# Head outputs of groups 0 to 5 stored by token and brought back through DMA transposes; partial value products from two terms

## The chip, the core and the metric

The kernel runs on one core of a Trainium2 chip, in one launch. The metric is the device time of that launch in microseconds (us). TensorE (PE) does the matmuls and the weight loads before them (PEld), VectorE (DVE) and ScalarE (ACT) do elementwise work, GpSimd (POOL) hardly works here, and SyncE (SP) issues every DMA.

## The reference

```
xn = layernorm(x)                                  # x: 2048 tokens x 640
q, k, v = split(xn @ wqkv)                         # 32 heads of 20
p = softmax(q k^T / sqrt(20))                      # no mask, 2048 x 2048 per head
s = concat_heads(p @ v) @ wo
u = gelu(einsum("sd,sf->df", layernorm(xn), w1) + b1)   # a perceptron over tokens, F = 1536
g = silu((u @ w2 + b2)^T)
out = x + s * g
```

All tensors are bf16.

## The kernel before

**A planner writes the order.** `schedule()` runs when the kernel is built. It keeps an estimated clock for every engine, and at each step appends one instruction to one engine's list, the best candidate by priority and estimated readiness. Every instruction names the slots that it reads and writes, and `_add` (L81) turns these into semaphore waits. So the order on each engine is fixed at build time, and an engine that waits holds up all that stands behind it on its list. All DMAs stand on SP's list. They take eight semaphores ("lanes") in turn, and a DMA also waits for the one before it on its lane, which is the eighth DMA back (L171).

**Passes.** The heads are cut into 8 groups of 4, the queries into 4 blocks of 512. Groups 0 to 5 run as passes 0 to 23, four passes each; groups 6 and 7 alternate in passes 24 to 31. A pass has 16 key chunks x 4 heads, which makes 64 tiles of scores, 128 keys x 512 queries each; the whole run has 2048. PE computes a tile into one PSUM bank (L1114). The exponential of it is taken by one of two engines:

- ACT (L1143) takes two or three banks in one instruction and writes `pt_sb`.
- DVE takes four tiles of one key chunk at a time. L1154 turns each into an integer that is read as a bf16 power of two, and L1178 adds three constants to all four, so that there are four terms whose weighted sum approximates the exponential. The weights sit in the values: `v_sb` for term 0 and the scaled copies `vs_sb` for terms 1 to 3.

The value products (L1194) gather a pass in PSUM bank 6, 21 rows per head (a row of ones gives the denominator). A tile from ACT costs one value product, a tile from DVE four. `emit_pv` may take all terms of a DVE chunk that are left, or, with `PARTS = (2, 1)`, two or one of them as soon as these are ready:

```
for n in self.PARTS:
    if n < left or (n == left and not whole):
        pv.append(mk([], [(quads[0], n)]))
```

How many tiles go to DVE is not set anywhere: the planner gives DVE a chunk when DVE's estimated clock has room. In this kernel it is 480 tiles of 2048.

**End of a pass** (`ep_steps`, L1283). Four DVE instructions: L1288 transposes bank 6 in blocks of 32x32 into `tr_sb`, so that tokens lie on partitions; L1294 takes the reciprocal of the denominators; L1299 multiplies and writes `on_sb` (one buffer); L1301 transposes `on_sb` back into a slot of `stage_sb`. SP then stores the slot to the scratch `oT_scratch_dram`, 128 KB in rows of one feature (L1305).

**Reload.** When pass 23 is done, ten DMAs (L802) bring the 480 features of groups 0 to 5 into `oT_sb`, which is the space of `xnT_sb`. Groups 6 and 7 are brought back pass by pass. The output projection (L829, and L834 for the last block) reads `oT_sb` as weights, a block of tokens at a time, from pass 26 on; L844 multiplies with the gate, L854 adds x, L863 stores. The four last token blocks are done after the last pass (L1453, L1455, L1457, L1460).

**Work between the passes.** The projections for later groups, the perceptron and its elementwise steps are jobs that the planner sets between tiles of scores when their planned pass has come. The second matmul of the perceptron (L557 with `regB`) takes `w2` in eight pieces of 768 KB, loaded into two halves of `regA` (L693): a piece can be loaded once PE is through with the piece two before it, and PE waits for it when it comes to it. The SP list around the reload is: store of pass 23, ten reload DMAs, a `w2` piece, store of pass 24, four small reloads, a `w2` piece, and so on.

**Other lines that the prediction names.** L440 loads the second bias by single elements: 2048 pieces of 2 bytes. L583 stores projected q and k from the three slots of `qs_sb`, L622 loads them by head for the next group. L1209 is a filler matmul that adds zeros, put in where the planner expects PE to sit idle.

Of the kernel before, what the change touches and what calls it, by code (L numbers as in the profile page):

```python
# [10 lines left out]
P = 128  # L11
# [235 lines left out]
class _Kern:  # L247
    D = 640
    H = 32
    DH = 20  # L250
# [30 lines left out]
    NTILE, NLIVE, EARLY = 8, 3, True  # L281
    QC = ((0.5, 3.0), (3.2, 6.4), (9.0, 13.5), (14.0, 18.0), (19.0, 22.0))
    LAG_D, LAG_J = 99.0, 99.0
    PARTS = (2, 1)
    V1A, V1B = 0.8, 4.0

    def __init__(self, nc, A_x, A_wqkv, A_wo, B_w1, B_b1, B_w2, B_b2, out):
# [13 lines left out]
    def build(self):  # L301
        nc = self.nc
        pr = self.prog
        S, NB, FC = self.S, self.NB, self.FC
        es = ExitStack()
        with es:
            E = es.enter_context
            bf, f32, u16 = dt.bfloat16, dt.float32, dt.uint16
            t = {}

            def sb(name, shape, d):
                t[name] = E(nc.sbuf_tensor(name, shape, d))
# [12 lines left out]
            sb("pt_sb", [P, self.RP, 512], bf)  # L325
            sb("dt_sb", [P, self.NTILE, 4, 512], u16)
            sb("zt_sb", [P, 2, 2, self.D], bf)
            sb("tr_sb", [P, 512], f32)
            sb("on_sb", [P, 16, 32], bf)
            sb("rden_sb", [P, 16], f32)  # L330
            sb("stage_sb", [P, 3, 512], bf)
            sb("idb_sb", [P, P], bf)
            sb("zw_sb", [P, 32], bf)
            sb("bst_sb", [P, NB, 12], f32)
            sb("st_sb", [P, 8, NB], f32)
            sb("cst_sb", [P, 4], f32)
            sb("b1h_sb", [P, FC], f32)
            sb("b2h_sb", [P, NB], f32)
            sb("bload_sb", [P, FC + NB], bf)
            t["ps_all"] = E(nc.psum_tensor("ps_all", [P, 4096], f32))  # L340
            t["qk_dram"] = nc.dram_tensor("qk_scratch_dram", [2, 560, S], bf)
            t["oT_dram"] = nc.dram_tensor("oT_scratch_dram", [8 * P, S], bf)
            sems = {}
            for e in ("pe", "act", "dve", "pool", "sp"):
                sems[e] = E(nc.semaphore(f"sem_{e}"))
            for i in range(pr.n_lanes):
                sems[f"d{i}"] = E(nc.semaphore(f"sem_d{i}"))
            self.t = t
            self.schedule()
            pr.final_waits()  # L350
            pr.emit(sems)

    def schedule(self):
# [10 lines left out]
        idb_sb, bst_sb, st_sb, cst_sb = t["idb_sb"], t["bst_sb"], t["st_sb"], t["cst_sb"]  # L364
        b1h_sb, b2h_sb, bload_sb = t["b1h_sb"], t["b2h_sb"], t["bload_sb"]
        ps_all, oT_dram, qk_dram, qs_sb = t["ps_all"], t["oT_dram"], t["qk_dram"], t["qs_sb"]
        PROW = 4096
        A_x, A_wqkv, A_wo, B_w1, B_b1, B_w2, B_b2, out = (self.A_x, self.A_wqkv, self.A_wo, self.B_w1,
                                                          self.B_b1, self.B_w2, self.B_b2, self.out)
# [425 lines left out]
        def oT_loads(f0, f1, col0, n, rd, wr, nm):  # L795
            steps = []
            for (c, r, h, o, nh, m) in pieces(f0, f1):
                d = oT_sb[r:r + nh * m, c, col0:col0 + n]
                sr = bass.AP(oT_dram, (32 * h + 1 + o) * S + col0, [[32 * S, nh], [S, m], [1, n]])
                ws = S_(f"{wr}_{c}_{r}")  # L800
                oT_slots.setdefault((wr, c), []).append(ws)
                steps.append(("dma", lambda e, d=d, sr=sr: e.dma_start(d, sr), rd, [ws], f"{nm}_{c}_{r}", nh * m * n * 2, xall))  # L802
            return steps

        xall = [S_(f"xT{dc}_{gb}") for dc in range(5) for gb in range(4)]

        def reload_steps():
            return oT_loads(0, 480, 0, S, [S_(f"oTd{G}") for G in range(6)], "oTa", "oTload") + [("tag", "oT")]

        def reload6_steps(p):  # L810
            def make(bk):
# [471 lines left out]
        def ep_steps(q):  # L1283
# [6 lines left out]
            def okacc():  # L1290
# [7 lines left out]
            nout = bass.AP(on_sb, 1, [[512, P], [32, 16], [1, DH]])  # L1298
            steps.append(("dve", lambda e: e.tensor_tensor(nout, nin, rin, ALU.mult), [S_("tr"), S_("rden")],  # L1299
                          [S_("on")], f"epm{q}", dv(320)))  # L1300
            steps.append(("dve", lambda e: e.transpose(stage_sb[:, s_, :], on_sb[:, :, :].rearrange("p a b -> p (a b)")),  # L1301
                          [S_("on")], [S_(f"stage{s_}")], f"epb{q}", 627.0))
            if not last_pass:
                dst = oT_dram[G * P:(G + 1) * P, p * 512:(p + 1) * 512]
                steps.append(("dma", lambda e, dst=dst, src=stage_sb[:, s_, :]: e.dma_start(dst, src),  # L1305
                              [S_(f"stage{s_}")], [S_(f"oTd{G}") if G < L6 else S_(f"oTd{G}_{p}")], f"oTst{q}", 131072))
            steps.append(("tag", f"ep{q}"))
            return steps

# [1 line left out]
        for i, (b0, nb) in enumerate(LN):  # L1311
            rq = () if i < 2 else (f"xn{LN[i - 1][0] + LN[i - 1][1] - 1}",)
            add_job(f"ln{b0}", ln_steps(b0, nb), rq, 20.0 + b0 / 4.0)
        pads = []
        for g in range(GH):
            pads.append(("dma", lambda e, g=g: e.dma_start(qk_sb[32 * g + DH:32 * g + 32, 1, :, :],
# [502 lines left out]
```

## Time and profile before

| what | value |
|---|---|
| time, median of 15 runs | 771.12 us (769.99 to 774.75) |
| the profiled execution | 771.59 us, span 769.8 us |
| busy share of the span | PE 96%, DVE 94%, ACT 96%, POOL 2% |
| granted TensorE clock | 0.998 |
| ACT exponentials (L1143) | 666 instructions, 718.7 us busy |
| DVE exponentials (L1154, L1178) | 480 and 360 instructions, 322.0 and 238.6 us busy |
| DVE at the end of a pass (L1288, L1294, L1299, L1301) | 32 each, 22.7 + 7.7 + 15.5 + 22.6 us busy |
| DMA | 51,623 packets, 41.47 MB; q1, the queue of SP, busy 17.6% |

The profile shows one execution. Span is the time from its first to its last instruction; 1.8 us of the execution lie around it. Busy time counts overlapping instructions of an engine once, so a group's busy time can be less than count times mean. "Idle before" is the time that an engine stood still ahead of a group, with the instruction that ended the wait. PE's busy time is no measure of how full it is, since matmuls are pipelined.

### The profile page before, as it was taken

What the parts mean: (1) busy time and instruction counts of PE and PEld (TensorE: products, weight loads), DVE (VectorE), ACT (ScalarE), POOL (GpSimd) and SP (SyncE); (2) the same over time, 40 slices, a digit from 0 to 9 for tenths busy, and PEclk for the clock granted to TensorE, in tenths of its full rate; (3) what the DMA queues carried; (4) which work ended last, traced back from release to release, by engine and by line L of the source; (5) the groups of instructions that cost most, each with busy time, mean ns of one, the idle gap of its engine ahead of it and who ended that gap; (6) DMA issues with size and microseconds to landing.
All of it is one profiled execution on the core that took longest, in us unless ns stands there. A gap on an engine that the chain in (4) does not pass through costs nothing.

```text
span 769.8 us, 22726 instructions
## 1 busy us (share of the span) xinstructions
PE 738.4 (96%) x10124; PEld 246.8 (32%) x10124; DVE 724.9 (94%) x1362; ACT 740.9 (96%) x707; POOL 12.7 (2%) x18
## 2 busy tenths in 40 slices
PE   9999999999999999998999999999999999999998
PEld 4433322222332323332223332332333333333332
DVE  7889999989999999989999999999999999999997
ACT  4999999999999999999999999999999999999993
POOL 3110000000000000000000000000000000000000
PEclk9999999999999999999999999999999999999999
DMA  9231101001120203012010003110323111040011
GB/s 265 71 72 48 46 22 39 22 16 32 37 63 15 77 15 94 9 33 75 10 46 22 26 10 103 40 55 9 100 74 117 55 54 54 3 149 26 33 46 69
DMA packets 51623, 41.47 MB, mean 54 GB/s; under 512 B 6229, under 2 KB 49877, under 8 KB 51477
## 3 DMA queue, kind: packets, MB, share of 16 engines
q1 hardware_dynamic: 51525, 40.02, 17.6%
q8 instruction: 79, 1.29, 0.7%
q14 instruction: 19, 0.16, 0.1%
HBM read 28.34 MB, written 11.27 MB: 51 GB/s over the span
## 4 chain that ended last, share of the span: by engine, by line
ACT 74%; PE 18%; DVE 6%; DMA 1%; SPq 0%; issue 0%; POOL 0%
ACT pt_sb L1143 72%; PE ps_all L1114 6%; PE ps_all L1194 6%; PE ps_all L557 5%; DVE dt_sb L1154 2%; DVE dt_sb L1178 1%; PE ps_all L829 1%; ACT zt_sb L752 1%; DMA regA<-in_A_x_dram 1%; ACT zt_sb L747 1%; DVE regC L1453 0%; DVE bst_sb L472 0%; PE ps_all L542 0%; DVE bst_sb L474 0%; DVE qs_sb L944 0%
## 5 line engine op out<-in xcount | busy, mean ns | idle before, releaser
L1143 ACT ACTIVATE pt_sb<-ps_all 128x1024 bf16<-128x1024 f32 (+1 forms) x666 | 718.7, 1221 | 4.7 <-PE ps_all L1114 3.2
L1154 DVE TENSOR_SCALAR dt_sb<-ps_all 128x512 uint16<-128x512 f32 x480 | 322.0, 682 | 26.2 <-PE ps_all L1114 24.0
L1114 PE MATMUL ps_all<-qk_sb 32*128 32x512 bf16 x2048 | 295.2, 385 | 22.6 <-ACT pt_sb L1143 19.9
L1178 DVE TENSOR_SCALAR dt_sb<-dt_sb 128x2048 uint16<-128x2048 uint16 x360 | 238.6, 686 | 1.5
L1114 PEld LDWEIGHTS ps_all<-qk_sb 32*128 32x128 bf16 x2048 | 75.5, 91 | 273.2 <-ACT pt_sb L1143 181.9
L1194 PE MATMUL ps_all<-dt_sb,vs_sb 128*21 128x512 bf16 x1440 | 129.0, 385 | 1.7 <-DVE dt_sb L1178 0.9
L1194 PE MATMUL ps_all<-pt_sb,v_sb 128*21 128x512 bf16 x1568 | 123.6, 383 | 0.0
L557 PE MATMUL ps_all<-regB,regA 128*32 128x128 bf16 (+1 forms) x1536 | 69.4, 301 | 0.0
L557 PE MATMUL ps_all<-regC,regA 128*32 128x512 bf16 (+1 forms) x1536 | 68.4, 301 | 0.4 <-DVE qs_sb L947 0.2
L1194 PEld LDWEIGHTS ps_all<-dt_sb,vs_sb 128*21 128x21 bf16 x1440 | 33.0, 91 | 58.4 <-issue 25.3
L557 PE MATMUL ps_all<-xnT_sb,wqk_sb 128*32 128x512 bf16 x640 | 51.0, 381 | 0.0
L1194 PE MATMUL ps_all<-dt_sb,v_sb 128*21 128x512 bf16 x480 | 47.9, 388 | 0.4 <-DVE tr_sb L1288 0.3
L1194 PEld LDWEIGHTS ps_all<-pt_sb,v_sb 128*21 128x21 bf16 x1568 | 29.0, 91 | 44.1 <-issue 35.7
L557 PEld LDWEIGHTS ps_all<-regB,regA 128*32 128x32 bf16 x1536 | 29.2, 96 | 27.2 <-issue 12.7
L557 PEld LDWEIGHTS ps_all<-regC,regA 128*32 128x32 bf16 x1536 | 28.5, 96 | 26.9 <-issue 12.7
L829 PE MATMUL ps_all<-wv_sb,xnT_sb 128*128 128x128 bf16 (+3 forms) x160 | 30.0, 303 | 0.0
L1288 DVE STREAM_TRANSPOSE tr_sb<-ps_all 128x512 f32<-128x512 f32 x32 | 22.7, 710 | 1.1 <-PE ps_all L1194 1.1
L557 PE MATMUL ps_all<-wv_sb,xnT_sb 128*32 128x480 bf16 x320 | 22.7, 369 | 0.2 <-DVE qs_sb L947 0.2
L1301 DVE STREAM_TRANSPOSE stage_sb<-on_sb 128x512 bf16<-128x512 bf16 x32 | 22.6, 705 | 0.1
L557 PEld LDWEIGHTS ps_all<-xnT_sb,wqk_sb 128*32 128x32 bf16 x640 | 15.2, 96 | 16.6 <-issue 6.3
L1194 PEld LDWEIGHTS ps_all<-dt_sb,v_sb 128*21 128x21 bf16 x480 | 12.5, 91 | 22.6 <-issue 16.4
L726 DVE TENSOR_SCALAR zt_sb<-ps_all,b2h_sb 128x512 bf16<-128x512 f32 (+1 forms) x32 | 17.1, 545 | 0.7 <-PE ps_all L557 0.4
(73 smaller groups left out, 312.8 us busy)
## 6 DMA issues: line engine op xcount, KB each, us to landing
regA<-in_B_w_dram SPq DMA_DIRECT2D x6, 1024.0 KB
regA<-in_B_w_dram SPq DMA_DIRECT2D x8, 768.0 KB
regA<-in_A_x_dram SPq DMA_DIRECT2D x7, 640.0 KB
qk_sb<-qk_scratch_dram SPq DMA_DIRECT2D x56, 80.0 KB
qk_scratch_dram<-qs_sb SPq DMA_DIRECT2D x32, 128.0 KB
oT_scratch_dram<-stage_sb SPq DMA_DIRECT2D x31, 128.0 KB
out_dram<-regC SPq DMA_DIRECT2D x3, 640.0 KB
wqk_sb<-in_A_wqkv_dram SPq DMA_DIRECT2D x2, 480.0 KB
```

The lines of the kernel that those rows point to most:

```text
L557: fns.append(lambda e, c=c, e_=e_: e.matmul(oc(c, e_), lhsT[:, c:e_], rhs, start=start, stop=stop, tile_position=(0, c)))
L726: steps.append(("dve", lambda e, z=z, i=i, jj=jj: e.tensor_scalar(z[:, c0:c0 + n], ps(bk, n, i * n), 0.5, bias[:, jj:jj + 1], ALU.mult, AL ...
L747: steps.append(("act", lambda e: e.activation(tt_, tt_, AF.Tanh, scale=1.5957691216), [stt], [stt], f"th{j}", ac(640)))
L752: steps.append(("act", lambda e: e.activation(tt_, z, AF.Tanh), sz, [stt], f"th2_{j}", ac(640)))
L829: steps.append(("pe", lambda e, c=c, k=k: e.matmul(ap, oT_sb[0:k, c, b * 128:(b + 1) * 128], wo_ap[0:k, c, c0:c0 + n], start=(c == 0), sto ...
L1114: pr.pe(lambda e, outp=outp, lhsT=lhsT, rhs=rhs, g=g: e.matmul(outp, lhsT, rhs, start=True, stop=True, tile_position=(32 * g, 0)), reads=[ ...
L1143: tk = pr.act(lambda e: e.activation(outp, inp, AF.Exp, scale=math.log(2.0) / 128.0), reads=[bank_slot[b] for b in banks[:n]], writes=[S_( ...
L1154: tk = pr.dve(lambda e: e.tensor_scalar(w, src, WOFF, 0.0, ALU.add, ALU.max), reads=[bank_slot[bk]], writes=[S_(f"dt{d['tl'][0]}_{g}")], n ...
L1178: tk = pr.dve(lambda e: e.tensor_scalar(dst, src, dk, None, ALU.add), reads=[S_(f"dt{b0}_{g}") for g in range(4)], writes=[S_(f"dt{b}_{g}" ...
L1194: pr.pe(lambda e: e.matmul(outp, lhsT, rhs, start=(k == 0), stop=last, tile_position=(0, 32 * g)), reads=reads, writes=[bank_slot[AB]], na ...
L1288: steps.append(("dve", lambda e: e.transpose(tr_sb[:, :], ps(AB)), [bank_slot[AB]], [S_("tr")], f"epT{q}", 632.0))
L1301: steps.append(("dve", lambda e: e.transpose(stage_sb[:, s_, :], on_sb[:, :, :].rearrange("p a b -> p (a b)")), [S_("on")], [S_(f"stage{s_ ...
```

## The change

For groups 0 to 5 the transpose back (L1301) and the store of the stage slot (L1305) go. In their place four DMAs, one for each head of the group, store the 20 columns of `on_sb` by token to a new scratch `ok_scratch_dram` of 2048 tokens x 512 columns: 32 partitions x 16 blocks x 20 elements, so 512 pieces of 40 bytes each. One DMA early in the run fills the columns 480 to 511 of the scratch with zeros. The reload becomes 16 DMA transposes, each from 512 tokens x 128 columns to 128 partitions x 512 tokens, which need all stores. Groups 6 and 7 stay as they were. `PARTS` loses its 1, so a DVE chunk's terms are no longer taken one at a time. Since the planner decides again, the order on every engine changes from about 50 us into the run on.

```diff
-    PARTS = (2, 1)
+    PARTS = (2,)
...
+            t["ok_dram"] = nc.dram_tensor("ok_scratch_dram", [S, 512], bf)
...
         def reload_steps():
-            return oT_loads(0, 480, 0, S, [S_(f"oTd{G}") for G in range(6)], "oTa", "oTload") + [("tag", "oT")]
+            steps = []
+            for c in range(4):
+                for tb in range(NTB):
+                    ws = S_(f"oTa_{c}_{tb}")
+                    oT_slots.setdefault(("oTa", c), []).append(ws)
+                    d = oT_sb[:, c, tb * 512:(tb + 1) * 512]
+                    src = ok_dram[tb * 512:(tb + 1) * 512, c * 128:c * 128 + 128]
+                    steps.append(("dma", lambda e, d=d, src=src: e.dma_start_transpose(d, src),
+                                  [S_(f"okd{pass_of[(G, tb)]}_{g}") for G in range(L6) for g in range(GH)] + [S_("okz")], [ws],
+                                  f"oTt{c}_{tb}", 131072, xall))
+            return steps + [("tag", "oT")]
...
             steps.append(("dve", lambda e: e.tensor_tensor(nout, nin, rin, ALU.mult), [S_("tr"), S_("rden")],
                           [S_("on")], f"epm{q}", dv(320)))
+            if G < L6:
+                for g in range(GH):
+                    dst = bass.AP(ok_dram, p * 512 * 512 + G * 80 + g * DH, [[512, 32], [32 * 512, 16], [1, DH]])
+                    src = on_sb[32 * g:32 * g + 32, :, 1:1 + DH]
+                    steps.append(("dma", small(lambda e, dst=dst, src=src: e.dma_start(dst, src)), [S_("on")],
+                                  [S_(f"okd{q}_{g}")], f"okst{q}_{g}", 300000))
+                steps.append(("tag", f"ep{q}"))
+                return steps
             steps.append(("dve", lambda e: e.transpose(stage_sb[:, s_, :], on_sb[:, :, :].rearrange("p a b -> p (a b)")),
                           [S_("on")], [S_(f"stage{s_}")], f"epb{q}", 627.0))
...
+        okz = bass.AP(ok_dram, 480, [[512, 128], [128 * 512, NB], [1, 32]])
+        ozs = bass.AP(zw_sb, 0, [[32, P], [0, NB], [1, 32]])
+        add_job("okz", [("dma", lambda e: e.dma_start(okz, ozs), [S_("zw")], [S_("okz")], "okz", 131072), ("tag", "okz")],
+                ("qk0_0_3",), 41.0)
```

More of the change, by code (lines that the diff above doesn't have):

```diff
@@ L366, in schedule @@
         ps_all, oT_dram, qk_dram, qs_sb = t["ps_all"], t["oT_dram"], t["qk_dram"], t["qs_sb"]
+        ok_dram = t["ok_dram"]
         PROW = 4096
@@ L801, in oT_loads @@
                 oT_slots.setdefault((wr, c), []).append(ws)
-                steps.append(("dma", lambda e, d=d, sr=sr: e.dma_start(d, sr), rd, [ws], f"{nm}_{c}_{r}", nh * m * n * 2, xall))
+                steps.append(("dma", lambda e, d=d, sr=sr: e.dma_start(d, sr), rd, [ws], f"{nm}_{c}_{r}", nh * m * n * 2,
+                              xall + [S_(f"oTa_{c}_{tb}") for tb in range(NTB)] if c == 3 else xall))
             return steps
@@ L1305, in ep_steps @@
                 steps.append(("dma", lambda e, dst=dst, src=stage_sb[:, s_, :]: e.dma_start(dst, src),
-                              [S_(f"stage{s_}")], [S_(f"oTd{G}") if G < L6 else S_(f"oTd{G}_{p}")], f"oTst{q}", 131072))
+                              [S_(f"stage{s_}")], [S_(f"oTd{G}_{p}")], f"oTst{q}", 131072))
             steps.append(("tag", f"ep{q}"))
```

## The prediction

> **What bounds the kernel now.** First the chain of work that ended last, then the time by stretches, cut where ACT's unbroken row of exponentials begins and ends (columns after the stretch: its length, then busy us and instructions of PE, PEld, DVE, ACT, POOL, then TensorE clock, DMA share, GB/s).
>
> ```profile
> ACT 74%; PE 18%; DVE 6%; DMA 1%; SPq 0%; issue 0%; POOL 0%
> ```
> ```profile
> 37.62:756.40 718.78, 694.62 (x9789) 226.22 (x9781) 686.27 (x1243) 715.56 (x679) 3.53 (x2) 1.00 0.16 47
> ```
>
> ACT is idle for 3.2 us of these 718.8. The 37.6 us before are the loads and the first projections, the 13.4 us after are the last pass and the last four token blocks. DVE, with 686.3 us, is nearly as full, but the ends of its waits say who leads; so I read the groups by shape and the waits (who waited for what: us, times, longest).
>
> ```profile
> L1143 ACT ACTIVATE pt_sb<-ps_all 128x1024 bf16<-128x1024 f32 x428 | 430.7, 1070 | 2.6 <-PE ps_all L1114 1.5 <-PE ps_all L1194 0.8
> L1143 ACT ACTIVATE pt_sb<-ps_all 128x1536 bf16<-128x1536 f32 x237 | 354.6, 1496 | 2.1 <-PE ps_all L1114 1.7
> ```
> ```profile
> PEld ps_all L1114 <- ACT pt_sb L1143: 181.9, 427, 1.2
> ...
> DVE dt_sb L1154 <- PE ps_all L1114: 24.0, 52, 1.4
> ```
>
> PE's weight loads wait 181.9 us for ACT to free banks; ACT waits 4.7 us before exponentials in the whole run. So ACT sets the pace, PE has room, and DVE is worth time only so far as it takes tiles off ACT.
>
> **What the new order gives ACT.** Compared instruction by instruction, the two built programs are equal up to about 50 us, and the tail after the last exponential is equal in kind. DVE takes 484 tiles in place of 480, so ACT takes 1564 in place of 1568: 438 two-bank, 229 three-bank instructions and one single, in place of 428, 237 and one. Price: the two shapes differ by 512 columns and 1496 - 1070 = 426 ns, 0.832 ns a column. 1568 x 512 columns x 0.832 = 668.0 us; the remaining 50.7 of 718.7 us over 666 instructions are 76 ns each. After: 1564 x 512 x 0.832 = 666.2, plus 668 x 0.076 = 50.8, in all 717.0 us. ACT gains **1.6 us**, and this is on the path.
>
> **DVE.** 24 L1301 go; 4 L1154 and 3 L1178 come. What an instruction holds up is its pitch, less than its duration:
>
> ```profile
> 593.75 1.89 DVE L1178 TENSOR_SCALAR dt_sb<-dt_sb 128x2048 uint16<-128x2048 uint16 x3
> ...
> 600.44 0.71 DVE L1301 STREAM_TRANSPOSE stage_sb<-on_sb 128x512 bf16<-128x512 bf16 x1
> 601.07 0.65 DVE L1154 TENSOR_SCALAR dt_sb<-ps_all 128x512 uint16<-128x512 f32 x1
> ```
>
> Three L1178 in 1.89 us with 0.69 for the last make a pitch of 0.60; the transpose holds 601.07 - 600.44 = 0.63. So -24 x 0.63 + 7 x 0.60 = -10.9 us. That is off the path, except that a freer DVE can shorten ACT's 3.2 us of gaps. I take 0.2 us of it; bounds 0 and -3.2.
>
> **PE.** 16 more value products (four more DVE terms per moved tile, less its one) and 32 more fillers: by 129.0/1440 and 6.7/72 us each, 1.4 + 3.0 = 4.4 us, and without single terms fewer turns between scores and products. Hidden in the 181.9 us that PE waits for ACT; without that cover it would be the 4.4 us.
>
> **The stores by token.** Per pass four DMAs of 512 pieces of 40 bytes for one of 128 pieces of 1 KB. No row has 40-byte pieces to memory; the nearest are the bias load of 2048 two-byte pieces, and the old store. SP's list (start, duration), then the DMA packets of 19.0 to 20.4 us, nearly all from the bias loads:
>
> ```profile
> 13.90 4.15 SPq L440 DMA_DIRECT2D bload_sb<-in_B_b_dram  x1
> ...
> 577.19 0.35 SPq L1305 DMA_DIRECT2D oT_scratch_dram<-stage_sb  x1
> 579.30 7.25 SPq L802 DMA_DIRECT2D xnT_sb<-oT_scratch_dram  x10
> 596.35 0.40 SPq L693 DMA_DIRECT2D regA<-in_B_w_dram  x1
> ```
> ```profile
> DMA packets 1832, 0.01 MB, mean 8 GB/s; under 512 B 1831, under 2 KB 1831, under 8 KB 1831
> ...
> q1 hardware_dynamic: 1831, 0.00, 75.5%
> ```
>
> 4.15 us for 2048 pieces is 2.03 ns a piece on SP: 1.04 us a store, 4.2 a pass, 96 x 1.04 = 100 us in the run less 24 x 0.34. A small piece holds a DMA engine for 0.755 x 16 x 1.4 us / 1831 = 9.2 ns; the 1 KB pieces of the store at 601.17, 144 packets taking 17.2% of 16 engines in a 2.2 us window, 42 ns. So 2048 pieces on 16 engines take 1.2 to 5.4 us; I take 3. SP waits 279.7 us in all for L1301 alone, so it has room. Queued behind the stores are L583 (three slots of `qs_sb`, so two more evictions before DVE would wait), L622 (loaded ahead of its group) and the `w` pieces; 4 us is covered by each. The new wait is L1299's: it must not overwrite `on_sb` before the four stores of the pass before have landed, and behind it DVE's whole list stands. Stores of consecutive passes are at least 19.8 us apart on SP (376.22 to 396.06); 4.2 + 3 + 1.7 (the longest wait of the reload for a store) = 9 us. Cost **0**, with 10 us of cover; at 42 ns a piece still 0. The early zero fill is 2048 pieces too, 4.2 us on SP at some 50 us, ahead of loads first needed past 100 us: 0.
>
> [...]
>
> **The reload.** SP issues 16 transposes in place of ten loads, and the next `w2` piece stands behind them. PE's weight pieces: in this run one is first used at 598.13 and the next at 616.89.
>
> ```profile
> 598.13 1.68 PE L557 MATMUL ps_all<-regB,regA 128*32 128x512 bf16 x28
> ...
> 616.89 1.47 PE L557 MATMUL ps_all<-regB,regA 128*32 128x512 bf16 x24
> ```
>
> The new order puts these two uses 46 tiles earlier and 14 tiles earlier in the row of 2048 scores; at 718.8 / 2048 = 0.35 us a tile that is 582 and 612. Pass 23 ends at about the same tile, so its stores are issued until 581 and landed by 582.4. A piece takes 4 us from issue (596.35) to its last byte (about 600.3). So the transposes have 612 - 4 - 582.4, with one us to spare some **24 us**, before PE, and with it ACT, stands still. No row shows a transpose. Bounds for 16: moved at the rate of a `w2` piece (768 KB in some 2.9 us), 2 MB take 8 us; every 32 bytes a piece of its own (the built instruction names tiles of 16 rows, 16 x 2 bytes), 65,536 pieces x 9.2 ns / 16 = 38 us of data, or 133 us if SP issues each at 2.03 ns. I take one piece per source row of 256 bytes, 512 x 2.03 ns = 1.04 us each, **17 us**, near what the old reload took (issued from 579.3, its packets end at about 594.5). Within 24 us: cost 0. The projection reads the result only at 686.4.
>
> [...]
>
> **Sum.** Span 769.8 - 1.6 - 0.2 = 768.0, with the 1.8 us around it 769.8 for this execution; it stood 0.5 us above the median, so **769.3 us**. A measurement of this kernel can tell about 0.2%, 1.54 us, from no change: the forecast lies hardly past that edge.
>
> **The rivals.**
> - *Late weights* (slower): the transposes outlast their 24 us, so the `w2` piece behind them is late, PE stops at L557, scores stop, ACT starves. Decides from 1.5 us a transpose. At 38 us: 38 - 24 = 14 us, 783. At 133 us: 109 us, 878. [...] Against: the old reload's 15 us. Chance 0.30.
> - *Stores too slow* (slower): L1299 waits for stores that take over 19 us to land; each us beyond costs DVE up to 23 us in the run, of which the freed 10.9 are cover. At 20 us: 23 - 11 = 12, 781. Chance 0.06.
> - *Gain given back* (no change): the planner's new order leaves ACT 1 to 3 us more of gaps where its clocks are off, 770.5 to 772.5. Chance 0.10: its gaps are 3.2 us now, so its clocks are good.
> - *Gaps closed* (faster): DVE's room removes most of the 3.2 us, 767. Chance 0.06.
> - *The forecast*: ACT's 1.6 us, 0.48.
>
> **Range and chances.** The forecast alone: 768.0 to 771.0. The gaps closed set the low end, 766.5; the data bound of the transposes, 783, with the stores' 781 below it, the high end 785; what lies above (transposes issued in 32-byte pieces) is left out at about 0.13. Faster: 0.36 of the forecast's 0.48 and the 0.06, 0.42. Same: 0.11 and 0.06, 0.17. Slower: 0.30, 0.06, 0.04 and 0.01, 0.41.
>
> **What would show it.** ACT's L1143 busy at 717, its idle before it under 5 us; L1299 without idle time before it from a DMA; the `w2` piece issued before 608 us and no wait of PE at L557 for it; SP's transposes within 17 us. A wait of L557 for a DMA, or ACT idle near 610 us, makes the late weights right; idle before L1299 the stores.

## The result, and the profile after

The changed kernel takes 769.24 us (median of 13 runs, 768.62 to 770.16), the kernel before 771.61 us (65 runs, 769.8 to 774.96). The ratio is 0.9966, 95% interval 0.9956 to 0.9977: a gain of 2.4 us, and the forecast of 769.3 us is met. The profiled execution has a span of 767.8 us for 769.8.

In the changed file the lines lie lower: L1114, L1143, L1154, L1178, L1194, L1288, L1299 of before are now L1127, L1156, L1167, L1191, L1207, L1301, L1312; the stores by token are L1318, the transposes L818, the `w2` pieces L695 and their matmul L559. First the chain of work that ended last, and a stretch of ACT's row (columns as before; it ends 1.3 us short of the row):

```profile
ACT 61%; PE 33%; DVE 4%; DMA 1%; SPq 0%; issue 0%; POOL 0%
```
```profile
37.62:754.50 716.88, 694.87 (x9843) 221.77 (x9847) 677.99 (x1232) 714.60 (x682) 3.52 (x2) 1.00 0.20 47
```

ACT still leads the chain, but for 61% where it was 74%, and PE for 33% where it was 18%. Over the whole row (37.47 to 756.44 before, 38.06 to 755.78 now) DVE is busy for 677.6 us and not 686.5, and ACT stands still for 2.3 us and not 3.2; the DMA share is 4 points higher. Next ACT's exponentials, together and by shape, and the waits (who for whom: us, times, longest).

```profile
L1156 ACT ACTIVATE pt_sb<-ps_all 128x1024 bf16<-128x1024 f32 (+1 forms) x668 | 719.1, 1217 | 3.8 <-PE ps_all L1127 2.5
```
```profile
L1156 ACT ACTIVATE pt_sb<-ps_all 128x1024 bf16<-128x1024 f32 x438 | 440.3, 1071 | 1.3 <-PE ps_all L1127 0.6
L1156 ACT ACTIVATE pt_sb<-ps_all 128x1536 bf16<-128x1536 f32 x229 | 343.4, 1499 | 2.5 <-PE ps_all L1127 1.9
```
```profile
PEld ps_all L1127 <- ACT pt_sb L1156: 190.1, 437, 1.1
...
DVE dt_sb L1167 <- PE ps_all L1127: 25.9, 57, 1.4
```

The counts are those of the built program. The exponentials are busy for 719.1 us, 0.4 more than before, although four tiles went to DVE. PE waits for ACT 8 us more than before, in spite of its extra matmuls. DVE's multiply into `on_sb`, which has to wait for the four stores of the pass before, and SP's list around the reload, with PE's next weight piece:

```profile
L1312 DVE TENSOR_TENSOR on_sb<-tr_sb,rden_sb 128x320 bf16<-128x320 f32 x32 | 15.4, 482 | 0.1
```
```profile
575.76 1.94 SPq L1318 DMA_DIRECT2D ok_scratch_dram<-on_sb  x4
577.75 22.90 SPq L818 DMA_TRANSPOSE xnT_sb<-ok_scratch_dram  x16
600.75 0.53 SPq L695 DMA_DIRECT2D regA<-in_B_w_dram  x1
```
```profile
610.14 1.05 PE L559 MATMUL ps_all<-regB,regA 128*32 128x512 bf16 x16
```

L1312 waits 0.1 us in the whole run, so the stores land in time. The transposes hold SP for 22.9 us, to 600.65; the piece behind them is given 4 us, as in the prediction, and PE comes to it at 610.14. Reckoned from the first transpose there were 610.14 - 4 - 577.75 = 28.4 us, of which 22.9 are used: 5.5 us are left. In this trace the DMA engines are busy with the piece until about 605.2, 4.4 us after its issue, so the reserve is nearer 5 us.

**Where the 2.0 us of span come from.** ACT's row ran from 37.47 to 756.44 and now runs from 38.06 to 755.78: its start is 0.6 us later, its length 1.25 us less. What follows the last exponential was 769.8 - 756.44 = 13.36 us and is 767.8 - 755.78 = 12.02. So the row gives 1.25 and the tail 1.34, and the start takes 0.6.

The start is no part of the change: the two programs are equal up to about 50 us, the first exponential is already late by the 0.6 us (15.86 for 15.27), and in the profiled executions of the kernels below the row starts anywhere from 36.9 to 38.3 us, at 37.45, 37.37 and 37.69 in runs 1 to 3, which keep the changed kernel's order on PE and ACT.

The row's 1.25 us are mostly not the change either. The execution of before that was profiled ran at half the TensorE clock from 347.30 to 350.71 us (the windows are in the last section), and ACT's row stood there:

```profile
349.35 0.80 ACT L747 ACTIVATE zt_sb<-zt_sb 128x640 bf16<-128x640 bf16 x1
351.04 11.85 ACT L1143 ACTIVATE pt_sb<-ps_all 128x1024 bf16<-128x1024 f32 x11 [0.89 <-PE ps_all L1114]
```

L747 is ACT's work for the perceptron. The next instruction follows one of these after 0.63 us everywhere else in the two rows; here it came after 1.69. Without these 1.06 us the row of before would have been 717.9 us long; it is 717.7 in the changed kernel, and 717.6 in run 1, which has the same order. So of the two terms the tail is the one that holds at an equal clock. This rests on one profile of before.

The tail is seen on DVE, at the last pass; first before, then after (start, duration, in brackets what it waited for):

```profile
756.54 1.29 DVE L1178 TENSOR_SCALAR dt_sb<-dt_sb 128x2048 uint16<-128x2048 uint16 x2
758.91 0.72 DVE L1288 STREAM_TRANSPOSE tr_sb<-ps_all 128x512 f32<-128x512 f32 x1 [1.08 <-PE ps_all L1194]
```
```profile
757.09 0.72 DVE L1301 STREAM_TRANSPOSE tr_sb<-ps_all 128x512 f32<-128x512 f32 x1 [5.80 <-PE ps_all L1207]
```

Before, DVE's own last terms came at 757.83, after ACT's last exponential, and the end of the pass stood until PE had multiplied them. After, DVE has been idle for 5.8 us, and the last pass waits for ACT's tiles alone.

**What the row is made of.** From start to start, exponentials in a row take 903 ns for two banks and 1330 for three (medians in both traces 904 and 1330). The counts times these are the least length of the row; the rest I call "on top". Before: 421 x 0.903 + 229 x 1.330 = 684.7 us least; after 431 x 0.903 + 221 x 1.330 = 683.1. That is the 1.6 us of the forecast. But what lies on top grew from 14.9 us to 16.4 and took 1.5 of them back. ACT's other work and the last, single exponential, the remainder of the row, fell from 19.3 us to 18.2, and this is the stall of 1.06 us.

### The profile page after: what moved, and what is told of

Same layout as the page of the kernel before. It is cut to its first block, busy times and chain, and to the rows that moved or that the text cites. A ratio compares the mean times of both kernels' runs of the same rounds, so it can differ in the third digit from the quotient of the medians.

```text
span 767.8 us, 22884 instructions
## 1 busy us (share of the span) xinstructions
PE 737.5 (96%) x10168; PEld 241.7 (31%) x10168; DVE 714.7 (93%) x1345; ACT 740.6 (96%) x709; POOL 12.7 (2%) x18
## 4 chain that ended last, share of the span: by engine, by line
ACT 61%; PE 33%; DVE 4%; DMA 1%; SPq 0%; issue 0%; POOL 0%
ACT pt_sb L1156 59%; PE ps_all L1127 11%; PE ps_all L1207 10%; PE ps_all L559 7%; PE ps_all L842 3%; DVE dt_sb L1167 1%; ACT zt_sb L754 1%; DMA regA<-in_A_x_dram 1%; ACT zt_sb L749 1%; DVE dt_sb L1191 1%; PE ps_all L598 0%; PE ps_all L544 0%; DVE bst_sb L474 0%; DVE bst_sb L476 0%; DVE tr_sb L1301 0%
## 5 line engine op out<-in xcount | busy, mean ns | idle before, releaser
L1156 ACT ACTIVATE pt_sb<-ps_all 128x1024 bf16<-128x1024 f32 (+1 forms) x668 | 719.1, 1217 | 3.8 <-PE ps_all L1127 2.5
L1167 DVE TENSOR_SCALAR dt_sb<-ps_all 128x512 uint16<-128x512 f32 x484 | 323.6, 684 | 27.1 <-PE ps_all L1127 25.9
L1127 PE MATMUL ps_all<-qk_sb 32*128 32x512 bf16 x2048 | 294.2, 384 | 21.0 <-ACT pt_sb L1156 18.0
L1191 DVE TENSOR_SCALAR dt_sb<-dt_sb 128x2048 uint16<-128x2048 uint16 x363 | 240.2, 687 | 1.5
L1127 PEld LDWEIGHTS ps_all<-qk_sb 32*128 32x128 bf16 x2048 | 74.1, 91 | 281.8 <-ACT pt_sb L1156 190.1
L1207 PE MATMUL ps_all<-pt_sb,v_sb 128*21 128x512 bf16 x1564 | 124.9, 383 | 0.1
L1207 PE MATMUL ps_all<-dt_sb,vs_sb 128*21 128x512 bf16 x1452 | 118.9, 381 | 0.0
L559 PE MATMUL ps_all<-regC,regA 128*32 128x512 bf16 (+1 forms) x1536 | 67.7, 301 | 0.6 <-DVE qs_sb L957 0.6
L559 PE MATMUL ps_all<-regB,regA 128*32 128x128 bf16 (+1 forms) x1536 | 66.9, 301 | 0.0
L559 PE MATMUL ps_all<-xnT_sb,wqk_sb 128*32 128x512 bf16 x640 | 48.9, 382 | 0.0
L1207 PE MATMUL ps_all<-dt_sb,v_sb 128*21 128x512 bf16 x484 | 47.8, 385 | 0.8 <-DVE tr_sb L1301 0.7
L1207 PEld LDWEIGHTS ps_all<-pt_sb,v_sb 128*21 128x21 bf16 x1564 | 28.4, 91 | 54.4 <-issue 43.8
L1207 PEld LDWEIGHTS ps_all<-dt_sb,vs_sb 128*21 128x21 bf16 x1452 | 29.2, 91 | 30.8 <-issue 20.1
L559 PEld LDWEIGHTS ps_all<-regC,regA 128*32 128x32 bf16 x1536 | 28.3, 96 | 29.1 <-issue 14.3
L559 PEld LDWEIGHTS ps_all<-regB,regA 128*32 128x32 bf16 x1536 | 28.0, 96 | 27.5 <-issue 13.1
L842 PE MATMUL ps_all<-wv_sb,xnT_sb 128*128 128x512 bf16 (+3 forms) x160 | 29.8, 303 | 0.2 <-DVE regC L857 0.2
L1301 DVE STREAM_TRANSPOSE tr_sb<-ps_all 128x512 f32<-128x512 f32 x32 | 22.7, 710 | 6.0 <-PE ps_all L1207 6.0
L559 PE MATMUL ps_all<-wv_sb,xnT_sb 128*32 128x480 bf16 x320 | 21.1, 369 | 0.3 <-DVE v_sb L957 0.3
L559 PEld LDWEIGHTS ps_all<-xnT_sb,wqk_sb 128*32 128x32 bf16 x640 | 14.2, 95 | 20.5 <-issue 9.1
L1207 PEld LDWEIGHTS ps_all<-dt_sb,v_sb 128*21 128x21 bf16 x484 | 12.1, 90 | 25.1 <-issue 20.2
L842 PEld LDWEIGHTS ps_all<-wv_sb,xnT_sb 128*128 128x128 bf16 (+1 forms) x160 | 10.7, 97 | 15.4 <-issue 8.6
```

What stands on the lines that cost most here:

```text
L559: fns.append(lambda e, c=c, e_=e_: e.matmul(oc(c, e_), lhsT[:, c:e_], rhs, start=start, stop=stop, tile_position=(0, c)))
L842: steps.append(("pe", lambda e, c=c, k=k: e.matmul(ap, oT_sb[0:k, c, b * 128:(b + 1) * 128], wo_ap[0:k, c, c0:c0 + n], start=(c == 0), sto ...
L1127: pr.pe(lambda e, outp=outp, lhsT=lhsT, rhs=rhs, g=g: e.matmul(outp, lhsT, rhs, start=True, stop=True, tile_position=(32 * g, 0)), reads=[ ...
L1156: tk = pr.act(lambda e: e.activation(outp, inp, AF.Exp, scale=math.log(2.0) / 128.0), reads=[bank_slot[b] for b in banks[:n]], writes=[S_( ...
L1167: tk = pr.dve(lambda e: e.tensor_scalar(w, src, WOFF, 0.0, ALU.add, ALU.max), reads=[bank_slot[bk]], writes=[S_(f"dt{d['tl'][0]}_{g}")], n ...
L1191: tk = pr.dve(lambda e: e.tensor_scalar(dst, src, dk, None, ALU.add), reads=[S_(f"dt{b0}_{g}") for g in range(4)], writes=[S_(f"dt{b}_{g}" ...
```

## The experiments

Each was run against the kernel before on the same chip; ratios are to that. Differences "to the changed kernel" are between medians, mostly from different chips. On the four chips used here the runs of before at a mean clock of 0.999 or more have means of 770.54 to 770.77 us.

**1. The new DMAs made cheap.** The order of all instructions stays; each store writes 1 of its 16 blocks, and the transposes become plain loads of as many bytes. The kernel leaves out that data.

```diff
-                    src = ok_dram[tb * 512:(tb + 1) * 512, c * 128:c * 128 + 128]
-                    steps.append(("dma", lambda e, d=d, src=src: e.dma_start_transpose(d, src),
+                    src = qk_dram[0, c * 128:(c + 1) * 128, tb * 512:(tb + 1) * 512]
+                    steps.append(("dma", lambda e, d=d, src=src: e.dma_start(d, src),
...
-                    dst = bass.AP(ok_dram, p * 512 * 512 + G * 80 + g * DH, [[512, 32], [32 * 512, 16], [1, DH]])
-                    src = on_sb[32 * g:32 * g + 32, :, 1:1 + DH]
+                    dst = bass.AP(ok_dram, p * 512 * 512 + G * 80 + g * DH, [[512, 32], [1, DH]])
+                    src = on_sb[32 * g:32 * g + 32, 0, 1:1 + DH]
```

> The changed kernel with its order untouched on every engine, but each store by token cut to one of its 16 blocks (32 pieces in place of 512) and the 16 DMA transposes replaced by plain loads of the same size from another scratch; it leaves out that data, so the output is not the reference's. My theory, the new DMAs are hidden altogether: the time of the changed kernel, 769.2 us, within 1.5 us. Rival, the small stores and the transposes cost time by contention or by waits: 2 us or more faster, 767 or less.

768.91 us, ratio 0.9969 [0.9958, 0.9981], 0.3 us from the changed kernel. SP's list:

```profile
576.84 9.38 SPq L818 DMA_DIRECT2D xnT_sb<-qk_scratch_dram  x16
586.32 0.38 SPq L695 DMA_DIRECT2D regA<-in_B_w_dram  x1
```

The weight piece goes out 14 us earlier, and nothing clear is gained by it. The row is 717.6 us long and the tail 12.0, as in the changed kernel. The new DMAs cost nothing on the path that these runs can tell.

**2. The transposes issued twice.** The second round writes the same data, and the planner is told that it costs nothing, so the order is otherwise the same.

```diff
+            for c in range(4):
+                for tb in range(NTB):
+                    d = oT_sb[:, c, tb * 512:(tb + 1) * 512]
+                    src = ok_dram[tb * 512:(tb + 1) * 512, c * 128:c * 128 + 128]
+                    steps.append(("hid", lambda e, d=d, src=src: e.dma_start_transpose(d, src), [], [S_(f"oTa_{c}_{tb}")], f"again{c}_{tb}"))
```

> The changed kernel with its order untouched, but SP issues the 16 DMA transposes a second time right after the first. My theory, the weights behind them have some 5 us of cover left (the w2 piece is issued at 600.75, takes 4 us and is needed at 610.1) and beyond that PE stands: another 22.9 us on SP brings the piece to 627.6, so 16 to 18 us slower than the changed kernel, 785 to 787, with L559 waiting for a DMA and ACT idle near 610 us. Rival, SP or PE has other slack there, or a second round overlaps the first: less than 6 us slower.

789.62 us, ratio 1.0240 [1.0226, 1.0254], 20.4 us above the changed kernel. SP's list, then ACT:

```profile
576.99 23.42 SPq L818 DMA_TRANSPOSE xnT_sb<-ok_scratch_dram  x16
600.46 21.72 SPq L825 DMA_TRANSPOSE xnT_sb<-ok_scratch_dram  x16
622.27 0.53 SPq L695 DMA_DIRECT2D regA<-in_B_w_dram  x1
```
```profile
609.84 1.20 ACT L1169 ACTIVATE pt_sb<-ps_all 128x1024 bf16<-128x1024 f32 x1
630.07 1.45 ACT L1169 ACTIVATE pt_sb<-ps_all 128x1536 bf16<-128x1536 f32 x1 [19.03 <-PE ps_all L1140]
```

The piece is 21.5 us later, PE waits 18.1 us for it, ACT 19.0 us for scores. So the rival of the late weights is a real mechanism of this kernel, with a threshold; the changed kernel stays some 5 us short of it. The cost is 2.4 us above the 16 to 18 that I expected. Here the piece took 5.3 us from its issue to PE's start at 627.59, and the clock was at half from 612.24 to 636.13, 8.5 us beyond the wait, which may be the rest of the 20.4; the last section has more of it.

**3. DVE's transposes kept.** The changed kernel, with the 24 transposes back into `stage_sb` added again as work whose result nobody uses; the planner does not count them.

```diff
+                steps.append(("hidv", lambda e: e.transpose(stage_sb[:, s_, :], on_sb[:, :, :].rearrange("p a b -> p (a b)")),
+                              [S_("on")], [S_(f"stage{s_}")], f"epb{q}"))
```

> The changed kernel with its order untouched, but DVE again runs the 24 transposes back into the stage slots, which nothing reads, right after L1312. My theory, DVE's freed 15 us are what carries the four more tiles and the early end of the last pass: the 24 x 0.63 = 15.1 us press on a DVE that is idle some 27 us before L1167, so 1.5 to 8 us slower than the changed kernel, at or above the kernel before. Rival, the gain is an accident of the new order and DVE's room is not needed: the time of the changed kernel within 1 us.

780.03 us, ratio 1.0112 [1.0095, 1.0128], 10.8 us above the changed kernel; more than I expected. The waits, with L1135 the scores, L1164 ACT's and L1175 DVE's exponentials:

```profile
PEld ps_all L1135 <- DVE dt_sb L1175: 21.7, 67, 0.8
...
ACT pt_sb L1164 <- PE ps_all L1135: 7.6, 21, 0.7
```

PE waits 21.7 us for DVE where it waited 9.4, and ACT 7.6 us for scores where it waited 2.5. The tail is the same 12.0 us; the row's on top goes from 16.4 to 26.8 us, 10.4 of the 10.8. Of 24 x 0.63 = 15.1 us on DVE, seven tenths reach the end of the run. DVE was no idle bystander: this order, laid out without them, does not take 15 us more for nothing.

**4. Stores six times.** Five more sets of stores after each pass of groups 0 to 5, to another scratch.

```diff
+                for r in range(5):
+                    for g in range(GH):
+                        dst = bass.AP(ok2_dram, r * S * 512 + p * 512 * 512 + G * 80 + g * DH, [[512, 32], [32 * 512, 16], [1, DH]])
+                        src = on_sb[32 * g:32 * g + 32, :, 1:1 + DH]
+                        steps.append(("hid", small(lambda e, dst=dst, src=src: e.dma_start(dst, src)), [S_("on")],
+                                      [S_(f"okx{q}_{g}_{r}")], f"okx{q}_{g}_{r}"))
```

> The changed kernel with its order untouched, but SP issues every store by token five more times, into another scratch. My theory, the stores are hidden with room: 24 stores a pass take SP 24 x 0.48 = 11.6 us and land some 3 us later, 14 to 15 us of the 19.8 us between passes, so no wait of L1312 for a DMA and no change, within 1.5 us. Rival, pieces of 40 bytes crowd the DMA engines or SP's list: L1312, L585 or L624 late, 3 us or more slower.

900.17 us, ratio 1.1658 [1.1634, 1.1683]: a miss. SP's list, L1327 the four stores and L1333 the twenty more; then DVE's waits at its multiply:

```profile
274.59 1.92 SPq L1327 DMA_DIRECT2D ok_scratch_dram<-on_sb  x4
276.55 17.91 SPq L1333 DMA_DIRECT2D ok_scratch_dram<-on_sb  x20
```
```profile
DVE on_sb L1321 <- DMA qk_scratch_dram<-qs_sb: 30.6, 8, 8.0
DVE on_sb L1321 <- DMA ok_scratch_dram<-on_sb: 27.7, 8, 7.4
DVE on_sb L1321 <- DMA qk_sb<-qk_scratch_dram: 14.6, 3, 6.3
```

Four stores cost SP 0.48 us each, half of what I had taken. But the following twenty take 0.90 each: a DMA waits for the eighth before it, and 512 pieces of 40 bytes did not drain faster here, with the 16 DMA engines busy for 50 to over 90% of each us from 286 to 296. The 24 stores hold SP for 19.8 us, as long as the shortest pass of before, and what stands behind them is late: L1321 waits 73 us in all. My expectation reckoned the issue and forgot the drain. So the rival of the stores has a threshold too, somewhere between the present load and six times it.

**5 and 6. Each part alone.** The stores by token with `PARTS = (2, 1)` kept, and `PARTS = (2,)` alone.

```diff
-    PARTS = (2,)
+    PARTS = (2, 1)
```

> The changed kernel with PARTS back at (2, 1): the stores by token and the transposes alone. Its order gives DVE 492 tiles, ACT 1556 in 670 instructions. If the time follows ACT's share: 1556 x 512 x 0.832 + 670 x 76 ns = 713.7 us, 3.3 us less than the changed kernel's 717.0, so 766. My theory, which has DVE's room as the second limit (24 transposes put back cost 10.8 us): eight more tiles ask 8 x 0.60 + 6 x 0.60 = 8.4 us of DVE, so most of that is lost, 768 to 772, hence not clearly faster than the changed kernel. If PARTS were where the gain comes from: 771 or more.

> The kernel before with PARTS = (2,) alone, nothing stored by token. Its order gives DVE 476 tiles, ACT 1572 in 669 instructions. By ACT's share: 1572 x 512 x 0.832 + 669 x 76 ns = 720.5 us, 1.8 us more than before, 773. If PARTS were where the gain comes from: 769 to 770.

The first takes 796.6 us, ratio 1.0307 [1.0281, 1.0334], a miss by 25 us; the second 775.4, ratio 1.0045 [1.0028, 1.0063]. Neither half is faster than before; but each got an order of its own, so this does not show what a half is worth at an equal order. The first has 492 tiles on DVE, but ACT's row ends at 762.5 and the tail is 32.1 us. SP's list of it around the reload, and the wait on PE:

```profile
582.12 0.79 SPq L610 DMA_DIRECT2D qk_scratch_dram<-qs_sb  x2
582.95 3.75 SPq L624 DMA_DIRECT2D qk_sb<-qk_scratch_dram  x8
586.74 21.88 SPq L818 DMA_TRANSPOSE xnT_sb<-ok_scratch_dram  x16
608.67 0.59 SPq L1437 DMA_DIRECT2D wv_sb<-in_A_wo_dram  x1
609.37 1.50 SPq L1440 DMA_DIRECT2D wqk_sb<-in_A_wo_dram  x4
610.97 0.39 SPq L695 DMA_DIRECT2D regA<-in_B_w_dram  x1
```
```profile
PE ps_all L559 <- DMA regA<-in_B_w_dram: 8.4, 1, 8.4
```

Here the order has put ten other DMAs ahead of the transposes and five more between them and the piece: late weights again, without any doubling. And it leaves 120 matmuls of the output projection (L842) after the last score, where the changed kernel leaves 40; that is the long tail. The second has 476 tiles, a row on a par with before, and 67 such matmuls: a tail of 15.5 us for 13.4.

**7. More tiles on DVE.** One planner setting of the changed kernel.

```diff
-    LEND, LEND_MIN = 900.0, 3
+    LEND, LEND_MIN = 1100.0, 3
```

> The changed kernel with the planner's LEND at 1100 in place of 900, which lends DVE more tiles: 500, so 1548 for ACT in 671 instructions. By ACT's share: 710.4 us, 6.6 less than the changed kernel, 763. By DVE's room: 16 x 0.60 + 12 x 0.60 = 16.8 us more on DVE, more than the 15.1 us that cost 10.8 when the transposes were put back; against ACT's 6.6 us that is no gain, 769 to 776.

804.34 us, ratio 1.0410 [1.0383, 1.0437]: the direction was expected, the size not. ACT ends at 749.17, 6.6 us earlier, but 160 projection matmuls and 192 of the perceptron are left after the last score, and the tail is 53.2 us. What ACT wins was got by pushing PE's work behind the end.

**8. The planner's cost of a store halved.** This was meant to give another order with the same tiles. It does not: as built, the program is that of the changed kernel, instruction for instruction on every engine, and its trace has them in the same order. So the run repeats the changed kernel on another chip.

```diff
-                                  [S_(f"okd{q}_{g}")], f"okst{q}_{g}", 300000))
+                                  [S_(f"okd{q}_{g}")], f"okst{q}_{g}", 150000))
```

> The changed kernel with the planner's estimate for a store by token halved (150000 in place of 300000): the same instructions and the same 484 tiles and ACT shapes, in another order. It shows what the order alone is worth. If the tile counts decide: 769.2 within 1 us. If the order is a lottery: off by 2 us or more to either side.

769.24 us, ratio 0.9966 [0.9953, 0.9980], the same median. Row and tail are those of the changed kernel within half a us. That shows how well the gain repeats. What the order alone is worth it does not show; run 11, with the same 484 tiles in an order that does differ, is 9.6 us slower.

**9 and 10. Two attempts at a better version.** More tiles on DVE with no work left over.

```diff
-    SLACK, MINJ = 120.0, 640.0
+    SLACK, MINJ = 200.0, 640.0
...
-    LEND, LEND_MIN = 900.0, 3
+    LEND, LEND_MIN = 950.0, 3
```

The second attempt has the same `SLACK`, and `D_GUARD = 8` for 16 in place of the other line.

> The changed kernel with two of the planner's settings moved (SLACK 120 to 200, LEND 900 to 950), nothing else. DVE takes 496 tiles in place of 484, ACT 449 two-bank and 218 three-bank instructions; 40 projection matmuls are left after the last score, as in the changed kernel. Theory (the time is ACT's row plus a tail set by the work left over): row 1552 x 512 x 0.832 ns + 667 x 76 ns = 711.8 us for 717.0, tail unchanged: 769.2 - 5.2 = 764.0 us, within 763 to 765.5. Rival (DVE's list is the limit, as with the transposes kept): 12 tiles are 21 DVE instructions of 0.60 us, 12.6 us, in a row 5.2 us shorter; kept transposes took 15.1 us of DVE and cost 10.8, so 769.2 - 5.2 + 12 = 776 us. Second rival (PE's other work, now let in 80 ns later before a score, makes ACT wait): ACT idle before exponentials above 8 us, 768 or more.

> The changed kernel with SLACK 200 and D_GUARD 8 (for 120 and 16), nothing else. 496 tiles on DVE, ACT 432 two-bank, 229 three-bank; 39 projection matmuls after the last score, and the weight pieces near the reload used later (some 48 us of cover for the transposes, 35 in the changed kernel by the same count). Theory: row 711.4 us, 5.6 less than 717.0: 763.6 us, within 762.5 to 765.5. Rivals as in the run beside it: 776 if DVE's list is the limit, 768 or more if ACT is made to wait.

Both missed: 770.73 us, ratio 0.9985 [0.9970, 1.0000], and 778.49 us, ratio 1.0085 [1.0062, 1.0109]. The first, by shape:

```profile
L1156 ACT ACTIVATE pt_sb<-ps_all 128x1024 bf16<-128x1024 f32 x449 | 442.8, 1042 | 3.6 <-PE ps_all L1127 2.2 <-PE ps_all L1207 0.5
L1156 ACT ACTIVATE pt_sb<-ps_all 128x1536 bf16<-128x1536 f32 x218 | 321.1, 1473 | 2.0 <-PE ps_all L1127 1.1
```

The least length of its row is 441 x 0.903 + 210 x 1.330 = 677.5 us, 5.6 less than the changed kernel's, and 6.4 us more lie on top. Only 2 of them show as idle time. The rest is in exponentials that come late, each by a little: 323 of those that follow another start 10 ns or more after the least pitch, for 251 in the changed kernel. The mean durations are 29 and 26 ns *shorter* at the same time. An exponential that follows at once starts while the one before still ends, and lasts longer in the record (in the changed kernel 1088 ns in the mean for two banks, 1040 when it is over 60 ns late), so a shorter mean is no sign of faster work. Its chain of waits has ACT for 45%, PE for 39% and DVE for 14%. Work taken off one engine is waited for at another. The second attempt has 27.6 us on top and a tail of 14.5, with DVE's last products behind the last score as in the kernel before; why so much lies on top is open.

**11 and 12. Is it the setting or DVE's load?**

```diff
-    SLACK, MINJ = 120.0, 640.0
+    SLACK, MINJ = 160.0, 640.0
...
-    MLP_A, MLP_B = 2.6, 24.0
+    MLP_A, MLP_B = 2.6, 23.0
```

The second has `SLACK = 150.0` and nothing else.

> The changed kernel with SLACK 160 for 120 and the planned passes of the perceptron's jobs a little closer (MLP_B 23 for 24), which leaves DVE at 484 tiles and 40 projection matmuls after the last score; ACT has 431 two-bank and 234 three-bank exponentials. Start to start these take 903 and 1330 ns at the least in all runs so far, so that the least length of ACT's row stays within 0.2 us of the changed kernel's. What came on top in the row was 10.4 us in the changed kernel and 17.2 us with SLACK 200 and 496 tiles. Theory 1 (the 6.8 us are SLACK's, PE being allowed to be late for ACT): about half of it here, 3 us: 772 us. Theory 2 (they are the 12 more tiles on DVE, whose list was too full): 769.2 us as the changed kernel.

> The changed kernel with SLACK 150 for 120, nothing else: 488 tiles on DVE, 435 two-bank and 230 three-bank exponentials, 40 projection matmuls after the last score. The least length of ACT's row falls by 3 x 0.903 - 0.48 - 1.33 + 1.0 = about 1.9 us. Were nothing else to change: 767.3 us. Theory 1 gives 0.085 us per ns of SLACK back, 2.5 us: 769.8. Theory 2 gives 6.8 / 12 us a tile back, 2.3 us: 769.6. So both say no change from 769.2 within 1 us, and only the plain sum of tiles says a gain.

778.79 us, ratio 1.0095 [1.0073, 1.0116], and 772.94 us, ratio 1.0012 [0.9997, 1.0027]. Neither theory's number holds, and the question stays open, because each met something else. The first, on SP, PE and ACT:

```profile
582.67 23.42 SPq L818 DMA_TRANSPOSE xnT_sb<-ok_scratch_dram  x16
606.18 1.06 SPq L695 DMA_DIRECT2D regA<-in_B_w_dram  x1
```
```profile
612.32 2.95 PE L559 MATMUL ps_all<-regB,regA 128*32 128x512 bf16 x28 [4.66 <-DMA regA<-in_B_w_dram]
```
```profile
608.67 1.03 ACT L1156 ACTIVATE pt_sb<-ps_all 128x1024 bf16<-128x1024 f32 x1
615.64 4.63 ACT L1156 ACTIVATE pt_sb<-ps_all 128x1536 bf16<-128x1536 f32 x4 [5.94 <-PE ps_all L1127]
```

PE could have begun the piece at 612.32 - 4.66 = 607.66. From the first transpose that is 607.66 - 4 - 582.67 = 21.0 us, less than their 23.4: late weights for the third time. By this sum the piece is 2.4 us late; PE waited 4.66, because the piece took 6.1 us from its issue to PE's start, as in run 5, and not 4. Of 25.1 us on top in its row, 6.1 are this one stall. The second lost about 3.7 us on top between 439 and 450 us to a halved clock in the profiled execution; its five runs at full clock take 771.3 us in the mean, still 2 more than the changed kernel. So in run 11 a setting that moves the piece's use by a few us decides more than either theory; what the second lost at full clock is open.

One table of row and tail (us; "on top" is what the row takes beyond its least length, ACT's other work left out; in run 5 the stall for the late piece came just behind such work, so that 8.4 us of it stand in no column):

| kernel | DVE tiles | least | on top | ACT ends | tail | span |
|---|---|---|---|---|---|---|
| before | 480 | 684.7 | 14.9 | 756.4 | 13.4 | 769.8 |
| changed | 484 | 683.1 | 16.4 | 755.8 | 12.0 | 767.8 |
| 3, transposes kept | 484 | 683.1 | 26.8 | 766.7 | 12.0 | 778.7 |
| 5, `PARTS = (2, 1)` | 492 | 679.8 | 18.0 | 762.5 | 32.1 | 794.6 |
| 7, more tiles | 500 | 675.6 | 18.3 | 749.2 | 53.2 | 802.4 |
| 9, tuned | 496 | 677.5 | 22.8 | 756.4 | 11.9 | 768.2 |
| 10, tuned | 496 | 677.7 | 27.6 | 760.7 | 14.5 | 775.2 |
| 11, `SLACK` 160 | 484 | 682.1 | 25.1 | 763.9 | 12.1 | 776.0 |
| 12, `SLACK` 150 | 488 | 680.8 | 23.3 | 760.4 | 12.7 | 773.1 |

No version beat the changed kernel. The theory that runs 9 and 10 were to test, that the time follows the tiles once the tail is the same, fell with them: what lies on top moves by as much as the least length.

## Why the prediction was right, point by point

The number was met, but in good part by luck: the 1.6 us that it rests on were there and, as far as one profile of each kernel shows, were given back, and a shorter tail and a steadier clock, neither of them in the sum, brought the gain.

- *ACT's row gains 1.6 us.* Right by its tiles: the least length fell from 684.7 us to 683.1. As a gain of the run it did not come: 1.5 us more lie on top, and the row's 1.25 us are nearly all the stall at half clock in the profile of before. The sign that the prediction named for it, L1143 busy at 717 us, did not show: it is 719.1. The 76 ns for each instruction was mis-sized as a price: it is a mean over the row, with waits in it. The least price is 1330 - 903 = 427 ns for 512 columns, as predicted, and 49 ns an instruction.
- *Gaps shrink by 0.2 us.* As idle time of ACT they shrank by 0.9 us, 0.6 of it in the half-clock window of before. But idle time does not show the exponentials that come a little late, and the time on top grew.
- *The tail is equal in kind.* This step failed. The tail gave 1.34 us, more than the row, and at an equal clock nearly the whole gain. The same 40 projection matmuls are left after the last score, but the order of before left 32 others and the changed one 20, and before 16 of them were products of DVE's last terms, which came later than ACT's last tile.
- *The sum.* Its 1.8 us met a span gain of 2.0 that is made of other terms, with 0.6 us against it from a start that varies from execution to execution. And it set out from 0.5 us above the median of 15 runs, 771.12; the 65 runs have theirs at 771.61, where this execution stands, and from there the same sum gives 769.8.
- *DVE's 10.9 us lie off the path.* In the row no gain from them is seen; the tail is where DVE came off the path. As a price of DVE time zero was too low: 15.1 us put back cost 10.8.
- *PE's 4.4 us are hidden.* Right: PE waits more for ACT than before, 190.1 for 181.9 us.
- *Stores cost 0.* Right. 0.48 us each on SP and not 1.04; L1312 waits 0.1 us.
- *The transposes cost 0.* Right in outcome, mis-sized: 22.9 us and not 17, 1.43 each and not 1.04. The cover was 28.4 us, more than the 24 taken, because the transposes began at 577.75 and not at 582.4; against 24 there would have been 1 us to spare. The chance of 0.30 for late weights was not too high: three of the runs, two of them with nothing but a planner's setting moved, fell into it. No trace read then had a row for a transpose. As measured, a block of 128x128 takes 22.9 / 64 = 0.36 us, and the plain loads of the same bytes in run 1 hold SP for 9.38 us where the transposes hold it for 22.9.
- *Stores too slow; gain given back; gaps closed.* The first was excluded by L1312, with a threshold below six times the load. The second came about in the row, 1.5 us on top by the new order, as lateness and not as the idle gaps that it names; the time did not show it, because of the tail and the clock. The third did not: ACT still stands still for 2.3 us.

**A term that no step had.** The before kernel's runs differ by 5 us among themselves, and the granted clock goes with it. Of the 65 runs of it beside the experiments, 25 had a mean clock of 0.999 or more, and took 770.65 us in the mean; the other 40 took 772.66. All 13 runs of the changed kernel lie at 0.998 or above, 769.24 us in the mean, and so do the 10 of run 8. So about 1.4 us of the 2.4 are there at an undisturbed clock, which fits the 1.34 of the tail, and some 1.0 us is that the changed kernel hardly ever loses the clock. The profiled execution of before is one that lost it once. Why the changed order keeps it was not tried; what the traces show of it is the last section.

## What to carry to other kernels

Split such a run into the leading engine's row at its least pitch, what lies on top of it, and the tail after it: an order's tiles fix only the first, and more tiles on the helper engine were lost here (runs 7, 9 and 10) as soon as the other two terms moved. Where all DMAs stand in one list, reckon for each transfer that is late if it slips what is queued ahead of it and how many us are left; here some 5 us separated a gain from a loss of 6 to 20. When three engines are 94 to 96% busy, as in the kernel before, do not price a few us put on the second of them at zero; in the one test here they cost seven tenths of their length. Before a gain of 0.3% is put down to a row, look whether the profile that it is read from lost the clock.

## What the hardware showed that I had not expected

**Small pieces.** A store of 512 pieces of 40 bytes holds SP for 0.48 us while its lane is free, 0.94 ns a piece; twenty in a row drained at about 0.90 us each, 28 ns a piece on 16 engines. The bias load that I took as the nearest row had 2.03 ns a piece on SP and 9.2 ns on an engine: too dear for issue and too cheap for data.

**The clock goes down in steps, and not only after long waits.** In the traces the granted clock falls to 0.50 for 3.41 us or a multiple of it (10.24, 23.9). In three cases it falls while PE stands still for a weight piece, 2.5 to 3.8 us after PE stopped: in run 11 (a wait of 4.7 us) for 3.41 us, in run 5 (8.4 us) for 10.24, in run 2 (18.1 us) for 23.9, each time for 2.6 us or more beyond the wait. But it falls elsewhere too. Two windows of before, then two of run 12 (length, then busy us and instructions of PE, PEld, DVE, ACT, POOL, then clock, DMA share, GB/s):

```profile
343.89:347.30 3.41, 2.47 (x25) 0.58 (x17) 3.41 (x8) 3.41 (x4) 0.00 (x0) 1.00 0.00 0
347.30:350.71 3.41, 3.38 (x31) 0.96 (x33) 2.38 (x7) 2.85 (x3) 0.00 (x0) 0.50 0.04 15
```
```profile
436.32:439.73 3.41, 2.28 (x24) 0.70 (x25) 3.41 (x9) 3.41 (x5) 0.00 (x0) 1.00 0.00 0
439.73:449.97 10.24, 10.24 (x77) 1.70 (x73) 7.66 (x14) 7.48 (x7) 0.00 (x0) 0.50 0.76 152
```

In each pair PE was busy for 2.47 or 2.28 us of the 3.41 before the fall, waiting for full banks (in the first its weight loads waited 1.0 us for DVE and 0.9 for ACT) while ACT and DVE were busy throughout; at half clock PE, busy for 3.38 of 3.41 us and for all of 10.24, then becomes the limit, and ACT and DVE are idle for part of the time (busy 2.85 and 2.38 us of 3.41, 7.48 and 7.66 of 10.24). Run 4, with many falls (a mean clock of 0.936), is left aside. In the six falls within the rows of before and of runs 5, 7, 10 and 12, with no long wait before them, PE was idle for 0.9 to 1.4 us of the 3.41 ahead, a quarter to two fifths by the profile's busy time. By their number PE's matmuls were further down, since busy time is no measure of how full PE is (the 2048 matmuls of L1114 last 385 ns in the mean, 788 us together, within 295 us of busy time): 24 to 29 in such a window, for some 45 in the mean of the run (10,124 in 769.8 us). Not every such window is followed by a fall: in the changed kernel the one that ends at 461.9, with 1.0 us of idle and 29 matmuls, is not. So these traces do not show what sets off a fall, nor why the mean clock of one program differs from run to run (25 of the 65 runs of before at 0.999 or more, 40 below); no run here tests it.
